# Attention and two MLPs on one core: values in two scaled fp16 parts, raw loads on POOL's queue, a lag of four

## The chip, the cores and the metric

The kernel runs on 1 core of a Trainium2 chip. The metric is the device time of one execution in microseconds (us), from the host's single launch; lower is better. The engines are named as the profile names them: PE (TensorE matmul), PEld (TensorE weight load), DVE (VectorE), ACT (ScalarE), POOL (GpSimd) and SP (SyncE, which here only issues transfers).

## The reference, cut to what matters

```python
# q, k, v: (4, 8, 576, 64) float32; s: (4, 8, 576)
scores = 1/sqrt(64) * q @ k.T                       # per batch and head
bias = minimum(-(cum[i] - cum[j]), 0)               # cum = cumsum(max(s, 0))
scores = where(j > i, -1e9, scores + bias)
attn = exp(scores - rowmax); attn /= sum(attn) + 1e-9
x = (attn @ v) -> (2304 tokens, 512)
h = x @ moe_w_in   (512 x 2048);  x = (h * tanh(softplus(h))) @ moe_w_out
h = x @ moe2_w_in  (512 x 2048);  out = (h * sigmoid(1.702 h)) @ moe2_w_out
```

The weights of both MLPs come as 8-byte numbers, which the kernel turns into float32 itself.

## The kernel before

Every product is made from parts of lower precision: a float32 operand is split into a high part and a remainder, and the partial products are added in PSUM.

**Attention.** There are 4 batches `b` of 8 heads, and 5 row tiles `i` per batch (four of 128 rows and one of 64, which takes two heads at a time). A *step* is a few heads of one row tile (`steps`, 104 of them, 26 a batch; 2, 4, 8, 8 and 4 steps for `i` = 0 to 4). A *group* is `(b, i, half of the heads)`, 40 of them; its raw keys, queries and values are loaded by `load_group` (three transfers, L133, on SP's queue) and prepared by `split_items`: PE transposes (L157), ACT and DVE split into parts.

`tick()` emits one step: scores (`do_qk`, L289 and L294 on PE), row minimum with the bias (`do_max`, L307 on DVE), `do_exp` (L111 on ACT), `do_hilo`, which splits the scaled probabilities into two fp16 parts (L333 ACT, L334 DVE) and transposes both by a DMA transpose on SP's queue (L338, tile `pt`). It also emits some items of the prepare queue `prep_q` for later groups, and then `do_av` of the step that lies `LAG` ticks back. The load of group `gi + 3` and the preparing of group `gi + 2` are emitted while group `gi` runs.

In `do_av` the values are there in three bf16 parts (L187 ACT, L189 DVE, L193 ACT, L194 POOL). For each 128 keys and head the high part of the probabilities is multiplied with all three parts (L357, 192 columns) and the low part with the first two (L361, 128 columns): 480 such pairs in all. The outputs of two heads share a PSUM bank, the only one of pool `ps_o`; L366 (DVE) adds the parts of each pair of heads. After the last step of a tile `norm_tile` divides by the sums (L379, L380 DVE, L381 POOL), and `emit_tile` transposes and splits the tile into the first MLP's input `xh`, `EDEL` ticks later.

**First MLP, first layer, among the ticks.** Unit `u` is 256 tokens. `first_layer` runs 16 blocks of weights on a unit (L530 to L532, three products a weight tile), and `slot_a` emits ticks between them, spread evenly. The first unit can start when its 256 tokens are done. A weight tile is loaded by `load_w` (L499 for the first layer, 512 KB, on SP's queue) and split by ACT, DVE and POOL (L514 to L526); loads begin after the fourth tick, one a tick. The last two units run after attention.

**The rest.** From about 443 us on come the second layer of the first MLP (L530 to L532 with `acc`) and the second MLP (L792). They are not touched by the change.

The framework puts each engine's instructions in an order of its own (by readiness in its own model, among those whose buffers are free) and inserts the waits; at run time each engine and each issuing queue works in that order.

Of the kernel before, what the change touches and what calls it, by code (L numbers as in the profile page):

```python
# [16 lines left out]
DRAM = bass.MemoryType.DRAM  # L17
BIG = 1.0e9
PSC = 32768.0
PH = 3  # L20
PS_ = 4
PO = 1
QW = 2
VB = 11
MA = 5
MBB = 4
NRAW = 2
LGC = 3
HLB = 3
PB = 2  # L30
RB = 1
XTB = 2
PTB = 4
WAH = 4
ES = 6
PG = 4
WT = 3
XH = 3
UE = 2
# [4 lines left out]
A0 = 4  # L44
A1 = 11
EDEL = 4
LAG = 3


@with_exitstack  # L50
def attention_moe_moe_kernel(
# [65 lines left out]
    def switch_set(name):  # L117
# [3 lines left out]
        del since[:]  # L121
        gate_ins[0] = p.ins


    raw = {}
# [23 lines left out]
    def split_items(b, i, g):  # L149
        n = min(128, S - 128 * i)  # L150
        hold = {}

        def flip(src, nm, off):
            ps = ps_s.tile([128, 512], F32, tag="s", name=nm)
            for hl in range(HG):
                o = hl * 128 + off(hl)
                nc.tensor.transpose(ps[:, o:o + n], src[:n, hl].rearrange("p w d -> p (w d)"), ident[:n, :n])  # L157
            return ps.rearrange("p (h t) -> p h t", h=HG)

        def kT():  # L160
# [23 lines left out]
        def v1():  # L184
            vr = raw[b, i, g][2]
            vt[b, i, g] = vv = v_p.tile([128, HG, 3, D], BF16, tag="v", name="v")
            nc.scalar.activation(out=vv[:n, :, 0, :], in_=vr[:n], func=AF.Copy)  # L187
            hold["vr"] = t = pp.tile([128, HG, D], F32, tag="res", name="res", bufs=RB)
            nc.vector.tensor_tensor(out=t[:n], in0=vr[:n], in1=vv[:n, :, 0, :], op=ALU.subtract)  # L189

        def v2():
            vv, t = vt[b, i, g], hold["vr"]
            nc.scalar.activation(out=vv[:n, :, 1, :], in_=t[:n], func=AF.Copy)  # L193
            nc.gpsimd.tensor_tensor(out=vv[:n, :, 2, :], in0=t[:n], in1=vv[:n, :, 1, :], op=ALU.subtract)  # L194
            raw.pop((b, i, g))

        return [qT, v1, v2], kT

    def cum_setup():
        NB = B * H  # L200
# [123 lines left out]
    def do_hilo(x):  # L324
        L, mu, nb = x["L"], x["mu"], x["nb"]
        Lp = nb * 128
        w = mu * Lp
        hl = pp.tile([128, 2 * NTIL * 128], F16, tag="hl", name="hl", bufs=HLB)
        hv = hl[:, 0:2 * w].rearrange("p (a w) -> p a w", a=2)
        if Lp != L:  # L330
            nc.gpsimd.memset(hv[:, :, L:Lp], 0.0)
        wl = mu * L
        nc.scalar.activation(out=hv[:, 0, 0:wl], in_=x["P"][:, 0:wl], func=AF.Copy, scale=PSC)  # L333
        nc.vector.scalar_tensor_tensor(  # L334
            out=hv[:, 1, 0:wl], in0=x["P"][:, 0:wl], scalar=PSC, in1=hv[:, 0, 0:wl], op0=ALU.mult, op1=ALU.subtract
        )
        x["T"] = d = pt_p.tile([128, 2 * NTIL, 128], F16, tag="pt", name="pt")
        nc.sync.dma_start_transpose(out=d[:, 0:2 * mu * nb, :], in_=hl[:, 0:2 * w])  # L338

    ohold = {}  # L340

    def do_av(x):
        b, i, g, n, mu, nb = x["b"], x["i"], x["g"], x["n"], x["mu"], x["nb"]
        t = x["T"]
        for e, hs in enumerate(x["hs"]):
            j = x["j"] + e
            if j % 2 == 0:
                ohold["o"] = ps_o.tile([128, 2, 256], F32, tag="o", name="o")
            o = ohold["o"]
            two = len(hs) == 2  # L350
            for kb in range(i + 1):
                kn = min(128, S - 128 * kb)
                for a, h in enumerate(hs):
                    hl = h - g * HG
                    rows = slice(64 * a, 64 * a + n) if two else slice(0, 128)
                    vv = vt[b, kb, g][:kn, hl, :, :].rearrange("p c d -> p (c d)")
                    nc.tensor.matmul(  # L357
                        out=o[rows, j % 2, 0:3 * D], lhsT=t[:kn, e * nb + kb, rows], rhs=vv,
                        start=(kb == 0 and j % 2 == 0), stop=False, skip_group_check=True,
                    )  # L360
                    nc.tensor.matmul(  # L361
                        out=o[rows, j % 2, 0:2 * D], lhsT=t[:kn, (mu + e) * nb + kb, rows], rhs=vv[:, 0:2 * D],
                        start=False, stop=(kb == i), skip_group_check=True,
                    )
            if j % 2 == 1:
                nc.vector.tensor_reduce(  # L366
                    out=tl[b, i]["x"][:, j - 1:j + 1, :],
                    in_=o[:, :, 0:3 * D].rearrange("p u (c d) -> p u d c", c=3), axis=mybir.AxisListType.X, op=ALU.add,
                )

    xunit = {}
# [2 lines left out]
    def norm_tile(x):  # L374
# [4 lines left out]
        nc.vector.tensor_scalar(out=rs, in0=su, scalar1=1e-9, scalar2=PSC, op0=ALU.add, op1=ALU.mult)  # L379
# [25 lines left out]
        tok_done[0] = t0 + n  # L405

    prep_q = []
    late_k = {}

    def queue_prep(gi):  # L410
        if gi >= len(groups):
            return
        b, i, g = groups[gi]
        items, kT = split_items(b, i, g)
        if 0 < gi < len(groups) - 1:
            prep_q.append(lambda: load_group(*groups[gi + 1]))
        prep_q.extend(items)
        if i == 0 and b > 0:
            late_k[groups.index((b - 1, NTIL - 1, g))] = kT
        else:  # L420
            prep_q.append(kT)

    def pop_prep(m):
        for _ in range(min(m, len(prep_q))):
            prep_q.pop(0)()
# [6 lines left out]
    def tick():  # L432
# [12 lines left out]
        if t < NS:  # L445
# [7 lines left out]
            if last_of[gi] == t and x["i"] == NTIL - 1 and x["b"] + 1 < B:  # L453
                load_ck(x["b"] + 1, x["g"])
            do_hilo(x)
        pop_prep(npop)
        while avn[0] < NS and t - avn[0] >= LAG:
            x = steps[avn[0]]
# [7 lines left out]

    def attn_left():
        return nxt[0] < NS + LAG + EDEL

    tmp_n = [0]  # L470
    mo_b = [None]

    def tmp_pair(dt, nm):
        tmp_n[0] += 1
        p = mo_a if mo_b[0] is None or tmp_n[0] % (MA + MBB) < MA else mo_b[0]
        return p.tile([128, 1024], dt, tag="hs", name=nm)


    win_t, wout_t = {}, {}
# [4 lines left out]
    def load_w(pool, stage, lay, m, kind):  # L484
# [11 lines left out]
            src = (w1_in, w2_in, w1_out, w2_out)[lay + 2 * (kind == "out")]  # L496
        if kind == "in":
            n = src.shape[1] // NF
            nc.sync.dma_start(  # L499
                out=rv.rearrange("p (c f) -> p c f", c=KC),  # L500
                in_=src[:, m * n:(m + 1) * n].rearrange("(c p) f -> p c f", p=128),
            )
            win_t[lay, m] = t
        else:
            nc.sync.dma_start(out=rv, in_=src[m * 128:(m + 1) * 128, :])
# [52 lines left out]
    for g in range(2):  # L558
        load_ck(0, g)

    queue_prep(0)
    pop_prep(len(prep_q))
    queue_prep(1)
# [288 lines left out]
```

## Time and profile before

| | |
|---|---|
| Median of 3 runs | 1086.47 us (1085.53 to 1091.34) |
| Profiled execution, its own time | 1086.05 us |
| Span of the profiled execution | 1084.3 us |
| PE busy over the span | 1009.3 us (93%) |
| DVE, ACT, POOL busy | 582.8, 495.0, 231.0 us |
| Mean granted PE clock | 0.974 |

The span runs from the first to the last recorded instruction; 1.75 us of the execution's own time lie outside it. A busy share says how long an engine had an instruction in it. Register, branch and transfer-issuing instructions are not counted as busy; a transfer's issue shows as SPq or POOLq.

### The profile page before, as it was taken

How to read it: one execution, taken by the hardware profiler on the slowest of the kernel's cores; microseconds unless marked ns; L12 is line 12 of the kernel's file. 1: busy time of each engine (PE TensorE's matmuls, PEld its weight loads, DVE VectorE, ACT ScalarE, POOL GpSimd, SP SyncE). 2: the span in 40 equal slices, each digit the busy share in tenths (PEclk: the TensorE clock that was granted, in tenths of full speed). 3: DMA queues.
4: the chain of work that ended last, by engine and by line, in shares of the span. 5: the costliest groups of instructions: out<-in, count | busy, mean ns of one | idle time of the engine just before them, and what ended most of it. 6: DMA issues, size and time to landing. Idle time of an engine off the chain costs nothing. (4 is left out here: it accounts for less than half of the span.)

```text
span 1084.3 us, 16945 instructions
## 1 busy us (share of the span) xinstructions
PE 1009.3 (93%) x6392; PEld 877.5 (81%) x6392; DVE 582.8 (54%) x1090; ACT 495.0 (46%) x1050; POOL 231.0 (21%) x239
## 2 busy tenths in 40 slices
PE   4488799989998999999999998799999999999998
PEld 4477689879987888998888878688888888888897
DVE  6979776665555974676644566773322232232231
ACT  6768676676656973455312343442222222222221
POOL 4414220112010211566423254230100100100000
PEclk9598999999999999999999998899999999999999
DMA  9669977996599778689534565530300210210010
GB/s 252 147 157 239 208 169 147 185 230 153 129 176 207 164 165 201 216 308 388 183 129 137 165 194 166 175 116 1 117 1 1 78 40 1 59 39 1 20 40 20
DMA packets 236913, 149.63 MB, mean 138 GB/s; under 512 B 166880, under 2 KB 210912, under 8 KB 236832
## 3 DMA queue, kind: packets, MB, share of 16 engines
q1 hardware_dynamic: 231392, 139.12, 48.7%
q0 software_dynamic: 5440, 9.44, 3.0%
q8 instruction: 50, 0.82, 0.3%
q14 instruction: 31, 0.25, 0.1%
HBM read 89.20 MB, written 33.10 MB: 113 GB/s over the span
## 5 line engine op out<-in xcount | busy, mean ns | idle before, releaser
L530 PE MATMUL h<-xh,w 128*128 128x256 f32 (+1 forms) x768 | 249.5, 328 | 6.7 <-DVE z L779 5.4
L531 PE MATMUL h<-xh,w 128*128 128x256 f32 (+1 forms) x768 | 247.4, 322 | 0.0
L532 PE MATMUL h<-xh,w 128*128 128x256 f32 (+1 forms) x768 | 246.4, 322 | 1.0 <-POOL w L526 1.0
L792 PE MATMUL acc<-w,gh 128*128 128x512 f32 x576 | 177.6, 389 | 0.0
L530 PEld LDWEIGHTS h<-xh,w 128*128 128x128 f32 x768 | 145.5, 191 | 19.2 <-DVE z L779 5.9
L532 PEld LDWEIGHTS h<-xh,w 128*128 128x128 f32 x768 | 146.7, 191 | 11.6 <-POOL w L526 1.4
L531 PEld LDWEIGHTS h<-xh,w 128*128 128x128 f32 x768 | 146.6, 191 | 10.5
L779 DVE TENSOR_TENSOR z<-h,sg 128x512 f32<-128x512 f32 x72 | 49.7, 691 | 190.6 <-ACT sg L111 190.2
L111 ACT ACTIVATE sg<-h 128x512 f32<-128x512 f32 x72 | 42.9, 596 | 202.8 <-PE h L532 202.8
L792 PEld LDWEIGHTS acc<-w,gh 128*128 128x128 f32 x576 | 107.6, 188 | 21.9
L531 PE MATMUL acc<-gl,w 128*128 128x512 f32 (+1 forms) x320 | 118.9, 372 | 6.1 <-DVE gl L665 6.0
L526 POOL TENSOR_TENSOR w<-wst,w 128x512 fp32r<-128x512 f32 x64 | 90.8, 1420 | 143.3 <-ACT w L525 137.6
L530 PE MATMUL acc<-gh,w 128*128 128x512 f32 (+1 forms) x320 | 118.5, 371 | 0.0
L532 PE MATMUL acc<-gh,w 128*128 128x512 f32 (+1 forms) x320 | 116.9, 371 | 0.1
L792 PE MATMUL acc<-w,gl 128*128 128x512 f32 x288 | 112.0, 389 | 0.0
L111 ACT ACTIVATE P<-P,mx 128x128 f32<-128x128 f32 (+4 forms) x144 | 83.5, 581 | 34.1 <-DVE mx L307 33.5
L334 DVE SCALAR_TENSOR_TENSOR hl<-P,hl 128x512 f16<-128x512 f32 (+2 forms) x104 | 74.8, 720 | 39.8 <-ACT hl L333 39.3
L357 PE MATMUL o<-v,pt 128*128 128x192 bf16 (+2 forms) x480 | 73.0, 257 | 23.5 <-DMA pt<-hl 13.4
L289 PE MATMUL s<-kw,qw 128*128 128x288 f32 (+4 forms) x384 | 90.3, 347 | 2.0 <-DVE qw L180 1.0
L514 ACT ACTIVATE wst<-wst 128x512 f32<-128x512 f32 x64 | 43.7, 683 | 77.2 <-DMA wst<-in_moe_w_out_dram 39.0
L781 DVE TENSOR_TENSOR gl<-z,gh 128x512 fp32r<-128x512 f32 x72 | 50.5, 701 | 47.8 <-ACT gh L780 35.7
L531 PEld LDWEIGHTS acc<-gl,w 128*128 128x128 f32 x320 | 61.4, 192 | 17.2 <-DVE gl L665 7.3
(79 smaller groups left out, 1713.0 us busy)
## 6 DMA issues: line engine op xcount, KB each, us to landing
h_d<-hs SPq DMA_DIRECT2D x36, 512.0 KB, 3.8
hg<-h_d SPq DMA_DIRECT2D x36, 512.0 KB, 6.3
wst<-in_moe_w_in_dram SPq DMA_DIRECT2D x32, 512.0 KB, 4.4
wst<-in_moe_w_out_dram SPq DMA_DIRECT2D x32, 512.0 KB, 3.7
x_d<-x SPq DMA_DIRECT2D x36, 256.0 KB, 2.8
xh<-x_d POOLq DMA_DIRECT2D x16, 512.0 KB, 5.2
cp<-cum_d SPq DMA_DIRECT2D x16, 288.0 KB, 5.1
ck<-cum_d SPq DMA_DIRECT2D x6, 768.0 KB, 6.9
```

The lines of the kernel that those rows point to most:

```text
L111: i = nc.scalar.activation(out=out, in_=in_, func=func, **kw)
L289: nc.tensor.matmul(out=o, lhsT=qw[b, i, g][:, hl, w, :], rhs=kw[b, g][:, hl, c0:c1], start=(e == a == w == 0), stop=False, skip_group_chec ...
L334: nc.vector.scalar_tensor_tensor(out=hv[:, 1, 0:wl], in0=x["P"][:, 0:wl], scalar=PSC, in1=hv[:, 0, 0:wl], op0=ALU.mult, op1=ALU.subtract)
L357: nc.tensor.matmul(out=o[rows, j % 2, 0:3 * D], lhsT=t[:kn, e * nb + kb, rows], rhs=vv, start=(kb == 0 and j % 2 == 0), stop=False, skip_g ...
L514: nc.scalar.activation(out=y, in_=y, func=AF.Copy, scale=2.0 ** -112)
L526: nc.gpsimd.tensor_tensor(out=tl_, in0=y, in1=th, op=ALU.subtract)
L530: nc.tensor.matmul(out=outp, lhsT=hi_w, rhs=hi_x, start=start, stop=False, skip_group_check=True)
L531: nc.tensor.matmul(out=outp, lhsT=hi_w, rhs=lo_x, start=False, stop=False, skip_group_check=True)
L532: nc.tensor.matmul(out=outp, lhsT=lo_w, rhs=hi_x, start=False, stop=stop, skip_group_check=True)
L779: nc.vector.tensor_tensor(out=z, in0=ps, in1=sg, op=ALU.mult)
L781: nc.vector.tensor_tensor(out=gl, in0=z, in1=gh, op=ALU.subtract)
L792: nc.tensor.matmul(out=acc[tb], lhsT=gx[:, ts], rhs=w[:, wx, :], start=m == 0 and a == 0, stop=m == NF - 1 and a == 2, skip_group_check=True,)
```

## The change

- The values are kept in two fp16 parts, after being scaled by a factor per batch that brings the batch's largest absolute value to 16384. `norm_tile` takes the factor out again. The factor needs the whole batch's values: `vscale_load(b)` loads them once more in three chunks of 128 x 768 floats into slots of the `hs` buffers and takes their largest (DVE), and `vscale_set(b)` makes the factor (a PE transpose and small DVE operations). For batch 0 they come at the start, for the others as items of the prepare queue with groups `(3, 0)` and `(4, 0)` of the batch before.
- `do_av` multiplies the high probabilities with both parts (128 columns) and the low ones with the first (64 columns). Four heads share the PSUM bank, and one reduction on DVE serves four heads.
- The remainder of the values is one DVE operation; one ACT, one DVE and one POOL operation per group fall away. Within a group keys are prepared ahead of values; the values of the first two groups are split after the first step.
- `load_group` issues its three transfers from POOL's queue instead of SP's from the fifth group on (`PG = 4`).
- `LAG` goes from 3 to 4, the `pt` buffers from 4 to 5, the value tiles from 11 to 12, the raw value buffers from 2 to 3; the buffer `res` goes.
- A weight load of the first layer is ordered on SP's queue behind the last transpose emitted before it.

```diff
-            t = pp.tile([128, HG, w, D], F32, tag=nm, name=nm, bufs=3 if nm == "kraw" else 2)
-            nc.sync.dma_start(
+            t = pp.tile([128, HG, w, D], F32, tag=nm, name=nm, bufs=2 if nm == "qraw" else 3)
+            (nc.sync if groups.index((b, i, g)) < PG else nc.gpsimd).dma_start(
...
-            vt[b, i, g] = vv = v_p.tile([128, HG, 3, D], BF16, tag="v", name="v")
-            nc.scalar.activation(out=vv[:n, :, 0, :], in_=vr[:n], func=AF.Copy)
-            hold["vr"] = t = pp.tile([128, HG, D], F32, tag="res", name="res", bufs=RB)
-            nc.vector.tensor_tensor(out=t[:n], in0=vr[:n], in1=vv[:n, :, 0, :], op=ALU.subtract)
+            vt[b, i, g] = vv = v_p.tile([128, HG, 2, D], F16, tag="v", name="v")
+            nc.scalar.activation(out=vv[:n, :, 0, :], in_=vr[:n], func=AF.Copy, scale=vsc[b][:n, 0:1])
...
-            nc.scalar.activation(out=vv[:n, :, 1, :], in_=t[:n], func=AF.Copy)
-            nc.gpsimd.tensor_tensor(out=vv[:n, :, 2, :], in0=t[:n], in1=vv[:n, :, 1, :], op=ALU.subtract)
+            nc.vector.scalar_tensor_tensor(
+                out=vv[:n, :, 1, :], in0=raw.pop((b, i, g))[2][:n], scalar=vsc[b][:n, 0:1], in1=vv[:n, :, 0, :],
+                op0=ALU.mult, op1=ALU.subtract,
+            )
...
+    def vscale_load(b):
+        flat = v[b].rearrange("h t d -> (h t d)").rearrange("(p n) -> p n", p=128)
+        vmx[b] = m = sm_p.tile([128, VC + 1], F32, tag="vm", name="vm")
+        for c in range(VC):
+            t = tmp_pair(F32, "vl")[:, 0:VW]
+            nc.sync.dma_start(out=t, in_=flat[:, c * VW:(c + 1) * VW])
+            nc.vector.tensor_reduce(
+                out=m[:, c:c + 1], in_=t, axis=mybir.AxisListType.X, op=ALU.max, apply_absolute_value=True
+            )
...
-            if j % 2 == 0:
-                ohold["o"] = ps_o.tile([128, 2, 256], F32, tag="o", name="o")
+            if j % 4 == 0:
+                ohold["o"] = ps_o.tile([128, 4, 2 * D], F32, tag="o", name="o")
...
+            if lay == 0 and last_pt[0] is not None:
+                tc.add_manual_dep(ld.ins, last_pt[0].ins.name, order, reason="weights behind transposes")
...
+    vscale_load(0)
     queue_prep(0)
```

## Rows read from the trace of the kernel before

**Rows 1.** Windows by stage: length, busy us and count per engine, clock, DMA share, GB/s.

```profile
0.00:122.00 122.00, 83.63 (x589) 72.70 (x590) 101.19 (x216) 85.44 (x204) 44.62 (x55) 0.86 0.83 200
122.00:140.00 18.00, 11.11 (x132) 9.34 (x129) 10.78 (x37) 11.03 (x34) 1.55 (x3) 0.91 1.03 203
140.00:443.00 303.00, 288.96 (x2640) 266.17 (x2641) 192.60 (x494) 200.18 (x515) 47.97 (x65) 0.99 0.78 172
443.00:600.00 157.00, 156.91 (x811) 134.76 (x810) 93.12 (x97) 59.19 (x77) 78.48 (x64) 1.00 0.67 232
```

**Rows 2.** Waits of PE, 0 to 445 us: total us, times, longest.

```profile
PE qt L157 <- ACT qraw L141: 18.2, 7, 6.7
PE o L357 <- DMA pt<-hl: 13.4, 9, 2.9
PE qt L157 <- POOL qraw L139: 11.9, 4, 5.2
PE o L357 <- DVE x L366: 10.1, 6, 2.9
```

**Rows 3.** Timeline of PE at 160 us: start, duration, instruction.

```profile
160.04 0.25 PE L357 MATMUL o<-v,pt 128*128 128x192 bf16 x1
160.12 0.22 PE L361 MATMUL o<-v,pt 128*128 128x128 bf16 x1
160.17 0.25 PE L357 MATMUL o<-v,pt 128*128 128x192 bf16 x1
```

**Rows 4.** Windows of L361 alone: PE and PEld busy us (count), clock, DMA share, GB/s.

```profile
140.00:443.00 303.00, 49.25 (x360) 30.66 (x360) 0.99 0.78 172
...
200.00:240.00 40.00, 7.55 (x64) 4.76 (x64) 1.00 0.98 210
...
320.00:360.00 40.00, 6.38 (x56) 3.97 (x56) 1.00 0.93 200
```

**Rows 5.** Windows of 40 us, columns as in Rows 1.

```profile
0.00:40.00 40.00, 17.63 (x90) 15.68 (x90) 30.31 (x65) 26.87 (x67) 16.44 (x29) 0.89 0.95 241
40.00:80.00 40.00, 29.95 (x221) 25.93 (x222) 30.78 (x70) 26.11 (x67) 9.99 (x10) 0.77 0.51 125
80.00:120.00 40.00, 34.05 (x262) 29.18 (x262) 38.24 (x80) 31.17 (x69) 16.76 (x15) 0.91 1.01 230
...
200.00:240.00 40.00, 35.45 (x355) 31.93 (x354) 24.41 (x76) 26.07 (x68) 4.24 (x8) 1.00 0.98 210
...
320.00:360.00 40.00, 36.04 (x359) 33.22 (x358) 24.32 (x71) 27.07 (x76) 5.21 (x9) 1.00 0.93 200
```

**Rows 6.** Groups by line, whole span: busy us, mean ns, idle before.

```profile
L366 DVE TENSOR_REDUCE x<-o 128x128 f32<-128x384 f32 x72 | 39.7, 552 | 27.4 <-PE o L361 27.0
...
L194 POOL TENSOR_TENSOR v<-res,v 128x256 bf16<-128x256 f32 (+1 forms) x40 | 28.1, 703 | 103.3 <-ACT v L193 94.4 <-DVE x L366 4.0 <-PE s L294 3.1
...
L189 DVE TENSOR_TENSOR res<-vraw,v 128x256 f32<-128x256 f32 (+1 forms) x40 | 20.5, 512 | 12.5 <-POOL v L194 7.6 <-ACT v L187 4.3 <-issue 0.3
L193 ACT ACTIVATE v<-res 128x256 bf16<-128x256 f32 (+1 forms) x40 | 16.5, 411 | 3.6 <-DVE res L189 3.5
```

**Rows 7.** Issue durations by tile or line, ns: minimum, median, maximum.

```profile
L133 SPq DMA_DIRECT2D qraw<-in_q_dram x40: 368/532/1507, 1.7 to 378.2; - x40
...
L338 SPq DMA_TRANSPOSE pt<-hl x104: 1210/1284/6617, 24.4 to 422.2; - x104
...
L757 POOL DMA_DIRECT2D xh<-x_d x20: 716/716/922, 637.4 to 1024.1; - x20
```

**Rows 8.** Waits of POOL, 0 to 445 us.

```profile
POOL x L381 <- DVE x L366: 96.6, 17, 24.4
```

**Rows 9.** Timeline of SP at the start; first unit's first product.

```profile
5.94 1.05 SPq L499 DMA_DIRECT2D wst<-in_moe_w_in_dram  x2
...
24.42 3.94 SPq L338 DMA_TRANSPOSE pt<-hl  x1
...
L530 PE MATMUL h<-xh,w x64: 278/283/562, 66.3 to 121.6; 128*128 128x256 f32 x64
```

More of the change, by code (lines that the diff above doesn't have):

```diff
@@ L19 @@
 PSC = 32768.0
+VTOP = 16384.0
 PH = 3
@@ L23 @@
 QW = 2
-VB = 11
+VB = 12
 MA = 5
@@ L30 @@
 PB = 2
-RB = 1
 XTB = 2
-PTB = 4
+PTB = 5
 WAH = 4
@@ L36 @@
 PG = 4
+VT = 0
 WT = 3
@@ L46 @@
 EDEL = 4
-LAG = 3
+LAG = 4
 @with_exitstack
@@ L122, in switch_set, with tmp_pair @@
         gate_ins[0] = p.ins
+    tmp_n = [0]
+    mo_b = [None]
+    def tmp_pair(dt, nm):
+        tmp_n[0] += 1
+        p = mo_a if mo_b[0] is None or tmp_n[0] % (MA + MBB) < MA else mo_b[0]
+        return p.tile([128, 1024], dt, tag="hs", name=nm)
     raw = {}
@@ L184, in v1 @@
         def v1():
+            if b not in vsc:
+                vscale_set(b)
             vr = raw[b, i, g][2]
-            vt[b, i, g] = vv = v_p.tile([128, HG, 3, D], BF16, tag="v", name="v")
-            nc.scalar.activation(out=vv[:n, :, 0, :], in_=vr[:n], func=AF.Copy)
-            hold["vr"] = t = pp.tile([128, HG, D], F32, tag="res", name="res", bufs=RB)
-            nc.vector.tensor_tensor(out=t[:n], in0=vr[:n], in1=vv[:n, :, 0, :], op=ALU.subtract)
+            vt[b, i, g] = vv = v_p.tile([128, HG, 2, D], F16, tag="v", name="v")
@@ L191, in v2 @@
+            nc.scalar.activation(out=vv[:n, :, 0, :], in_=vr[:n], func=AF.Copy, scale=vsc[b][:n, 0:1])
         def v2():
-            vv, t = vt[b, i, g], hold["vr"]
-            nc.scalar.activation(out=vv[:n, :, 1, :], in_=t[:n], func=AF.Copy)
-            nc.gpsimd.tensor_tensor(out=vv[:n, :, 2, :], in0=t[:n], in1=vv[:n, :, 1, :], op=ALU.subtract)
-            raw.pop((b, i, g))
-        return [qT, v1, v2], kT
+            vv = vt[b, i, g]
+            nc.vector.scalar_tensor_tensor(
+                out=vv[:n, :, 1, :], in0=raw.pop((b, i, g))[2][:n], scalar=vsc[b][:n, 0:1], in1=vv[:n, :, 0, :],
+                op0=ALU.mult, op1=ALU.subtract,
+            )
@@ new lines, in split_items @@
+        return [qT], [v1, v2], kT
+    vsc, vmx = {}, {}
+    VC = 3
+    VW = H * S * D // 128 // VC
+    def vscale_load(b):
[7 more added lines that the diff above has]
+            )
+        nc.vector.tensor_reduce(out=m[:, VC:VC + 1], in_=m[:, 0:VC], axis=mybir.AxisListType.X, op=ALU.max)
@@ new lines, in vscale_set @@
+    def vscale_set(b):
+        m = vmx.pop(b)
+        w = pp.tile([128, 128], F32, tag="vw", name="vw", bufs=1)
+        nc.vector.tensor_copy(w, m[:, VC:VC + 1].to_broadcast([128, 128]))
+        ps = ps_s.tile([128, 512], F32, tag="s", name="vx")
+        nc.tensor.transpose(ps[:, 0:128], w, ident)
+        vsc[b] = t = sm_p.tile([128, 2], F32, tag="vs", name="vs")
+        nc.vector.tensor_reduce(out=t[:, 0:1], in_=ps[:, 0:128], axis=mybir.AxisListType.X, op=ALU.max)
+        nc.vector.tensor_scalar(
+            out=t[:, 0:1], in0=t[:, 0:1], scalar1=1.0e-30, scalar2=1.0 / VTOP, op0=ALU.max, op1=ALU.mult
+        )
+        nc.vector.reciprocal(t[:, 0:1], t[:, 0:1])
+        nc.vector.tensor_scalar(out=t[:, 1:2], in0=t[:, 0:1], scalar1=PSC, scalar2=None, op0=ALU.mult)
@@ L337, in do_hilo @@
         x["T"] = d = pt_p.tile([128, 2 * NTIL, 128], F16, tag="pt", name="pt")
-        nc.sync.dma_start_transpose(out=d[:, 0:2 * mu * nb, :], in_=hl[:, 0:2 * w])
+        last_pt[0] = nc.sync.dma_start_transpose(out=d[:, 0:2 * mu * nb, :], in_=hl[:, 0:2 * w])
     ohold = {}
+    last_pt = [None]
     def do_av(x):
@@ L357, in do_av @@
                     nc.tensor.matmul(
-                        out=o[rows, j % 2, 0:3 * D], lhsT=t[:kn, e * nb + kb, rows], rhs=vv,
-                        start=(kb == 0 and j % 2 == 0), stop=False, skip_group_check=True,
+                        out=o[rows, j % 4, :], lhsT=t[:kn, e * nb + kb, rows], rhs=vv,
+                        start=(kb == 0 and j % 4 == 0), stop=False, skip_group_check=True,
                     )
                     nc.tensor.matmul(
-                        out=o[rows, j % 2, 0:2 * D], lhsT=t[:kn, (mu + e) * nb + kb, rows], rhs=vv[:, 0:2 * D],
+                        out=o[rows, j % 4, 0:D], lhsT=t[:kn, (mu + e) * nb + kb, rows], rhs=vv[:, 0:D],
                         start=False, stop=(kb == i), skip_group_check=True,
                     )
-            if j % 2 == 1:
+            if j % 4 == 3:
                 nc.vector.tensor_reduce(
-                    out=tl[b, i]["x"][:, j - 1:j + 1, :],
-                    in_=o[:, :, 0:3 * D].rearrange("p u (c d) -> p u d c", c=3), axis=mybir.AxisListType.X, op=ALU.add,
+                    out=tl[b, i]["x"][:, j - 3:j + 1, :],
+                    in_=o.rearrange("p u (c d) -> p u d c", c=2), axis=mybir.AxisListType.X, op=ALU.add,
                 )
@@ L378, in norm_tile @@
         su = ts["sums"]
-        nc.vector.tensor_scalar(out=rs, in0=su, scalar1=1e-9, scalar2=PSC, op0=ALU.add, op1=ALU.mult)
+        nc.vector.tensor_scalar(out=rs, in0=su, scalar1=1e-9, scalar2=vsc[x["b"]][:, 1:2], op0=ALU.add, op1=ALU.mult)
         nc.vector.reciprocal(rs, rs)
@@ L407, in attention_moe_moe_kernel @@
     prep_q = []
+    v_first = []
     late_k = {}
+    VSTEP = {(3, 0): vscale_load, (4, 0): vscale_set}
     def queue_prep(gi):
@@ L420, in queue_prep @@
         else:
-            prep_q.append(kT)
+            items = items + [kT]
+        if gi < 2:
+            v_first.extend(vs)
+        else:
+            items = items + vs
+        if b + 1 < B and (i, g) in VSTEP:
+            items = items + [lambda: VSTEP[i, g](b + 1)]
+        prep_q.extend(items)
     def pop_prep(m):
@@ L455, in tick @@
             do_hilo(x)
+        if t == VT:
+            for f in v_first:
+                f()
         pop_prep(npop)
```

11 lines of the change are left out of this document (2 added, 9 removed).

## The prediction, on record before the result

> **What bounds the kernel now.** I read first the windows by stage, to find where PE, which is busy for 93% of the span, has room, and where another resource is full; then PE's waits inside the attention stage, PE's timeline for the pace of the products that the change shortens, and SP's and POOL's queues, between which transfers move.
>
> The change touches the attention stage alone, 0 to 443 us. Behind it PE is busy for 156.91 of the next 157 us, and the stages after that have no code of the change; I take them as shifted whole. So the question is how much earlier 443 us comes.
>
> That stage has two regimes [rows 1]. From 140 to 443 us PE is busy for 289.0 of 303 us at a granted clock of 0.99, with DVE at 193, ACT at 200 and the transfer engines at 0.78: PE bounds it, and 14 us are idle. From 0 to 140 us PE is busy for only 94.7 of 140 us. There the transfers are nearly full: 0.83 x 122 + 1.03 x 18 = 120 us of 140; DVE has 112. In finer slices the transfers are at 0.95 in the first 40 us, 0.51 in the next, 1.01 in the third, while DVE reaches 38.2 of 40 in the third [rows 5]. The half-idle second slice says that order and latency, not volume alone, hold the start. Two more slices, around the batch ends, look like the start: 200 to 240 (transfers 0.98, PE 35.45) and 320 to 360 (0.93, 36.04) [rows 5].
>
> PE's waits in the stage are few and named: for raw queries by way of the copies on ACT (18.2 us) and POOL (11.9), for `pt` from the DMA transpose (13.4), for the one `o` bank (10.1) [rows 2]. All four lie on things that the change moves.
>
> **The products, term one.** In the timeline a pair starts at 160.04, its second half at 160.12, the next pair at 160.17 [rows 3]: 0.13 us for 192 + 128 columns, which is one column a cycle at the 2.4 GHz level (133 ns: 80 and 53). After the change a pair is 128 + 64 columns. The 128-column half takes 53 ns instead of 80, a sure 27 ns. The 64-column half would be 27 ns by columns, but no row shows a 64-column product before another of this kind; if the weight load in front of each product sets a floor, that floor is at most the 53 ns that a 128-column one takes. So a pair saves 27 to 53 ns. I take 45: PEld is busy for 30.7 us over these 360 L361 loads [rows 4], 85 ns each, and two of them fit in the 133 ns of a pair only overlapped, so they have not been the limit, but how far below they go isn't seen.
>
> The Trainium skill ("TensorE: Matmul & The Clock Gate", Back-to-back issue gap) says that in a stream of weight load and product pairs a 128-column product takes about 81 ns. By it the new pair could hardly be under the old 133 ns, and this term would be nothing. The row shows 53 ns at 128 columns, so I go by the row.
>
> 360 of the 480 pairs lie behind 140 us, 64 and 56 of them in the two full slices at the batch ends [rows 4]. There, and for the 120 pairs of the first 140 us, PE isn't the bound and shorter products give no time. That leaves 240 x 45 ns = 11 us; if the batch ends gain too, 360 x 53 ns = 19 us; at the least, 240 x 27 ns = 6 us.
>
> **SP's queue and the waits, term two.** 36 groups x 3 = 108 issues leave SP. One takes 532 ns [rows 7], 57 us in all, and they stand in order with 104 transposes of 1.28 us (133 us). Each raw load ahead of a transpose holds it by its own issue and by whatever the load waits for. With a lag of four a transpose may also land one tick later. Of the 14 us that PE idles behind 140 us I give back 3; none to 8 bound it. The `o` bank now changes hands once for four heads.
>
> **The start, term three.** Today two weight tiles are issued at 5.94 us, ahead of most raw loads, and the first transpose's issue takes 3.94 us instead of the usual 1.28 because the transfers are full [rows 7, 9]. The new order puts all weight loads of the first layer behind transposes, and raw loads from the fifth group on leave SP. Against it: batch 0's values are read twice at the start. A batch is 8 x 576 x 64 x 4 B = 1.18 MB, 4.9 us at the 241 GB/s of the first slice [rows 5]; batch 1's second reading (b = 0, group (3, 0)) also falls before 140 us, so transfers rise from 120 to about 130 us. And the first unit starts one tick later: today's first product of it is at 66.3 us [rows 9], ten ticks in, so a tick is at most some 6 us, whose work isn't lost, since later ticks then have less. Best case: the stretch shrinks from 140 to the 130 us that its transfers need, 10 us. Worst: the two readings and a tick in full, 16 us lost. I take 6 us gained: the raw-query waits, 30 us in all [rows 2], of which at least 16 lie here since PE idles only 14 us later, come from the loads and copies that queue behind weights, and the 0.51 slice has room for the weights moved there.
>
> **The other engines, nothing.** ACT loses L193, 16.5 us; POOL loses L194, 28.1 us [rows 6]; none of it is on PE's path behind 140 us. DVE: 72 reductions of 552 ns over 384 elements become 36 over 512; by elements 736 ns, so 26.5 instead of 39.7 us. L189 is replaced by one operation on as many elements, 0.5 us as before. Twelve reductions over 768 elements cost 0.55 to 1.1 us each, 7 to 13 us, and the small operations for four factors perhaps 4 us, an estimate from five of about 0.2 us each. Together between -2 and +4 us on an engine that is 64% busy behind 140 us [rows 1]. PE gets four more transposes. If the cover of DVE's room were gone, as between 80 and 120 us, 4 us is what it costs.
>
> POOL takes 108 issues. The only ones in the trace take 716 ns [rows 7], 77 us; a raw load has shorter runs, so up to twice that, 155 us. POOL has 94 us of work in 443 today [rows 1], less 28, so 143 to 221 us afterwards: it fits, but in order. Behind each issue that waits for a raw buffer stand L526 (weights), L381 (normalising) and the memsets; and the loads stand behind these.
>
> The remaining readings of the values (b = 2, 3) are 2 x 4.9 us of transfers in the stretch whose mean share is 0.78 [rows 1], issued ahead of the full slices at the batch ends; I cost them at nothing as long as they land there, and at 10 us if they don't.
>
> **Sum.** Against the profiled execution's own 1086.05 us: 11 + 3 + 6 = 20 us less, 1066 us. The median shown is 1086.47, 0.4 above; the difference is inside rounding. A measurement of this kernel can tell about 0.5%, 5.4 us, from no change.
>
> **Rivals.**
> - *Raw loads come late from POOL (slower).* POOL stands at L381 for DVE's reduction 17 times, 96.6 us in all, up to 24.4 us in one [rows 8]. A raw load behind such a wait comes late, and PE then waits at the transposes (L157) as it does today at the start. It decides from 20/36 = 0.56 us of lateness per group on; at 0.8 us per group, 29 us, the time is 1066 + 29 = 1095. Against it: loads are emitted some three groups ahead, and a group is about 11 us (443/40), so a wait must be far longer than the usual 5.7 us (96.6/17) to matter. The Trainium skill ("DMA: Bandwidth & Descriptors", SWDGE vs HWDGE vs iDMA) adds that POOL writes its descriptors into SBUF, where DVE can lock it out; no row here prices that. 10%.
> - *Transfers are the bound after all.* Four readings, 4.7 MB, at 241 GB/s are 19.6 us; if they all fall into full stretches, they eat the gain: 1066 + 19.6 = about 1086. For it: four slices at 0.93 or more [rows 5]. Against: two of the four readings lie between the full stretches. 12%.
> - *The pair does not get shorter*, the floor being the weight load's: term one is nothing, and 1086 - 9 = 1077. Against: the 53 ns pace. 9%.
> - *More than forecast*: 19 us from the products, 8 from waits, 10 from the start: 1049. 9%.
> - *As forecast*, 1052 to 1078: 60%.
>
> The forecast and the two faster rivals lie below 1081, the transfers' case about the same as now, POOL's case above 1092: faster 0.78, same 0.12, slower 0.10. Leaving out the slower case and the outer half of the best one, and keeping the transfers' case, the range is 1049 to 1088.
>
> **What would show it.** Right: L357 and L361 pairs spaced at 80 to 110 ns; PE still above 95% behind the start; the first product of unit 0 no later than 66 us; the attention stage ending near 423 us. Wrong: PE idle in front of L157 for many groups with POOL's issue as what came last (the slower rival); transfers above 0.9 through the whole stage with waits for `pt` (the second); pairs at 130 ns (the third). A long wait for the scale factor of batch 0 before the first products with values would also undo the start's term.

## The result and the profile after

The changed kernel takes 1075.67 us (median of 7 runs, 1072.73 to 1080.59) against 1085.94 (7 runs) for the kernel before on the same chip: a ratio of 0.9896, 95% interval 0.9876 to 0.9916, so 1.04% or 11.3 us faster. Forecast was 1066, 20 us faster. The profiled execution took 1073.94 us.

Windows of the changed kernel by stage, columns as in [rows 1] (length, busy us and count of PE, PEld, DVE, ACT, POOL, clock, DMA share, GB/s), the last boundaries 10 us earlier than there:

```profile
0.00:122.00 122.00, 84.04 (x586) 71.82 (x587) 98.56 (x224) 78.77 (x189) 54.69 (x74) 0.78 0.95 219
122.00:140.00 18.00, 13.80 (x130) 11.61 (x128) 14.75 (x43) 16.29 (x47) 10.65 (x12) 0.91 1.09 252
140.00:433.00 293.00, 282.36 (x2703) 259.26 (x2703) 187.94 (x485) 194.47 (x483) 79.16 (x107) 0.99 0.85 189
433.00:590.00 157.00, 155.03 (x776) 131.76 (x775) 89.17 (x97) 58.72 (x75) 72.08 (x63) 1.00 0.64 225
```

POOL's busy time in these rows includes its issues of raw loads; on this engine, unlike on SP, an issue is counted as busy. PE is still the bound behind 140 us (282.4 of 293), but the transfers went from 0.83 to 0.95 in the first 122 us and from 0.78 to 0.85 behind them. The slices of 40 us, which answer to [rows 5], show where:

```profile
0.00:40.00 40.00, 20.91 (x120) 18.73 (x120) 26.82 (x72) 22.81 (x63) 18.48 (x36) 0.76 0.77 192
40.00:80.00 40.00, 29.05 (x205) 23.95 (x206) 36.33 (x74) 27.91 (x65) 14.94 (x16) 0.73 1.00 230
80.00:120.00 40.00, 32.08 (x245) 27.58 (x245) 35.08 (x80) 27.72 (x62) 20.62 (x23) 0.83 1.03 233
120.00:160.00 40.00, 35.80 (x346) 32.31 (x346) 31.55 (x82) 32.28 (x90) 19.37 (x24) 0.96 1.04 232
200.00:240.00 40.00, 36.24 (x365) 32.66 (x365) 27.32 (x83) 29.87 (x81) 14.16 (x22) 0.96 1.02 220
```

The half-empty slice of before (0.51 from 40 to 80 us) is gone: from 40 to 160 us the transfers are full without a gap. The fullness that stood in single slices has become one block, while the first slice fell from 0.95 to 0.77. PE is granted 0.78 of its clock over the first 122 us instead of 0.86 (both are means of the two levels), though it is as busy there as before, 84.0 us against 83.6; no run tells why.

PE's timeline of the changed kernel, to be held against [rows 3]:

```profile
170.16 0.22 PE L397 MATMUL o<-v,pt 128*128 128x128 f16 x1
170.22 0.19 PE L401 MATMUL o<-v,pt 128*128 128x64 f16 x1
170.25 0.22 PE L397 MATMUL o<-v,pt 128*128 128x128 f16 x1
170.30 0.19 PE L401 MATMUL o<-v,pt 128*128 128x64 f16 x1
```

The starts are 60, 30 and 50 ns apart. Over the pairs from 150 to 405 us that are followed at once by another one, the median spacing is 85 ns (164 pairs, halves of 57 and 28 ns; mean 89), where the kernel before has 138 ns (159 pairs, 83 and 56; mean 141): 53 ns less a pair.

PE's waits from 0 to 445 us in the changed kernel, columns as in [rows 2]:

```profile
PE o L397 <- DMA pt<-hl: 15.7, 11, 6.5
PE qt L166 <- POOL qraw L148: 5.2, 1, 5.2
...
PE o L397 <- DVE x L406: 3.3, 3, 2.9
PE qt L166 <- ACT qraw L150: 1.6, 2, 0.9
```

The waits for raw queries fell from 30.1 to 6.8 us and the one for the `o` bank from 10.1 to 3.3; the one for `pt` stayed (13.4 to 15.7). What the attention stage gave the later ones is seen in the line of the last two units' first layer, which run behind attention, before and after:

```profile
L530 PE MATMUL acc<-xh,w x128: 278/283/386, 424.8 to 472.7; 128*128 128x256 f32 x128
L576 PE MATMUL acc<-xh,w x128: 277/283/386, 408.7 to 456.2; 128*128 128x256 f32 x128
```

It begins at 408.7 us; in the kernel before at 424.8. The first product of the second MLP comes at 685.3 instead of 697.9, and the span ends at 1072.2 instead of 1084.3. So attention is 16.1 us shorter in the two profiles, and 3.6 us of them are lost again between the last two units and the second MLP, where no code changed.

### The profile page after: what moved, and what is told of

Its sections match the earlier page's. It is cut to its first block, busy times and chain, and to the rows that moved or that the text cites. A ratio compares the mean times of both kernels' runs of the same rounds, so it can differ in the third digit from the quotient of the medians.

```text
span 1072.2 us, 16959 instructions
## 1 busy us (share of the span) xinstructions
PE 1001.4 (93%) x6396; PEld 866.1 (81%) x6396; DVE 568.2 (53%) x1090; ACT 485.6 (45%) x1010; POOL 275.7 (26%) x307
## 4 chain that ended last, share of the span: by engine, by line
PE 49%; DMA 7%; DVE 4%; POOL 3%; issue 3%; ACT 2%; SPq 0%; ACTq 0%; POOLq 0%; DVEq 0%
PE acc L839 18%; PE h L576 7%; PE h L577 7%; PE h L578 7%; PE acc L578 3%; PE acc L577 3%; PE acc L576 3%; DMA wst<-in_moe_w_out_dram 2%; DMA wst<-in_moe_w_in_dram 2%; POOL w L572 2%; DMA x_d<-x 1%; DVE wst L565 1%; DVE gl L712 1%; DVE wst L562 1%; DMA kraw<-in_k_dram 1%
## 5 line engine op out<-in xcount | busy, mean ns | idle before, releaser
L576 PEld LDWEIGHTS h<-xh,w 128*128 128x128 f32 x768 | 147.7, 194 | 22.6 <-DVE z L826 6.1
L578 PEld LDWEIGHTS h<-xh,w 128*128 128x128 f32 x768 | 148.5, 193 | 11.5 <-POOL w L572 1.1
L577 PEld LDWEIGHTS h<-xh,w 128*128 128x128 f32 x768 | 148.5, 193 | 11.0 <-DVE xh L443 0.2
L112 ACT ACTIVATE P<-P,mx 128x128 f32<-128x128 f32 (+4 forms) x144 | 83.6, 582 | 32.4 <-DVE mx L346 31.9
L804 POOL DMA_DIRECT2D xh<-x_d x20 | 14.5, 729 | 285.3 <-PE h L578 197.4
L373 DVE SCALAR_TENSOR_TENSOR hl<-P,hl 128x512 f16<-128x512 f32 (+2 forms) x104 | 71.5, 688 | 30.5 <-ACT hl L372 30.2
L346 DVE CUSTOM_DVE_ANT_0 P<-s,ck 128x128 f32<-128x128 f32 (+3 forms) x128 | 59.2, 486 | 30.5 <-PE s L333 29.4
```

Source lines behind the costliest of these rows:

```text
L112: i = nc.scalar.activation(out=out, in_=in_, func=func, **kw)
L346: nc.vector.tensor_tensor_reduce(out=p[:, e * L + c0:e * L + c1], in0=x["S"][f][:, e * L:e * L + c1 - c0], in1=c[:, c0:c1], scale=1.0, sca ...
L373: nc.vector.scalar_tensor_tensor(out=hv[:, 1, 0:wl], in0=x["P"][:, 0:wl], scalar=PSC, in1=hv[:, 0, 0:wl], op0=ALU.mult, op1=ALU.subtract)
L576: nc.tensor.matmul(out=outp, lhsT=hi_w, rhs=hi_x, start=start, stop=False, skip_group_check=True)
L577: nc.tensor.matmul(out=outp, lhsT=hi_w, rhs=lo_x, start=False, stop=False, skip_group_check=True)
L578: nc.tensor.matmul(out=outp, lhsT=lo_w, rhs=hi_x, start=False, stop=stop, skip_group_check=True)
```

## The experiments

The theory after the result: the products and the queue gave what they could, and the second reading of the values, costed inside the start and at nothing for batches 2 and 3, ate the difference. The rivals: the products gave less than 11 us; the raw loads came late from POOL; the lag of four or the weight order cost something. Ratios are to the kernel before on the same chip (medians of 1089.16, 1086.97 and 1087.85 us in the three groups); differences of ratios are turned into us with 1087. The change itself was run only beside its own kernel before, so every comparison with it goes by way of that kernel. An interval reaches 0.002 to 0.004 to either side, so a difference is good to some 3 to 5 us.

| kernel | median, us | ratio, 95% |
|---|---|---|
| the change | 1075.67 | 0.9896 [0.9876, 0.9916] |
| e1_raw_on_sp | 1086.18 | 0.9977 [0.9957, 0.9996] |
| e2_low_part_128 | 1084.26 | 0.9968 [0.9950, 0.9986] |
| e3_no_second_reading | 1060.94 | 0.9746 [0.9713, 0.9779] |
| e4_lag3 | 1085.32 | 0.9952 [0.9926, 0.9978] |
| e5_no_weight_order | 1075.93 | 0.9903 [0.9877, 0.9930] |
| e6_before_raw_on_pool | 1083.47 | 0.9960 [0.9945, 0.9974] |
| e8_products_alone | 1089.78 | 1.0025 [1.0009, 1.0040] |
| e9_four_chunks | 1074.24 | 0.9873 [0.9837, 0.9909] |
| e12_transfers_only | 1072.20 | 0.9841 [0.9815, 0.9866] |
| e13_reduces_only | 1066.97 | 0.9796 [0.9766, 0.9827] |
| e14_products_no_reading | 1066.66 | 0.9808 [0.9788, 0.9828] |
| e10_constant_lag5 | 1059.26 | 0.9749 [0.9722, 0.9777] |

**Raw loads back on SP's queue.** The changed kernel, the lag and the rest kept.

```diff
-            (nc.sync if groups.index((b, i, g)) < PG else nc.gpsimd).dma_start(
+            nc.sync.dma_start(
```

> All raw loads go back to SP's queue; the rest of the change stays. Theory (transfers bound the start, PE the rest, and taking 108 issues from SP's queue is worth a few us of waits): the final units start 2 to 6 us later than in the changed kernel (408.7 us there), mostly lost behind 140 us, and the time is 1077 to 1082 us. Rival (raw loads come late from POOL and that is where the missing gain went): the final units start 4 us or more earlier and the time is below 1072 us.

It is 0.81% or 8.8 us slower than the change (0.9977 against 0.9896), more than the theory expected. The raw loads didn't come late from POOL; there they save time. What they cost is seen in the landings of the transposes, 0 to 440 us, by tile: issuing queue, form, count, median us from issue to landing. This kernel first, then the changed one:

```profile
pt<-hl SPq DMA_TRANSPOSE x104, 3.5
```

```profile
kraw<-in_k_dram POOLq DMA_DIRECT2D x28, 128.0 KB, 5.8
...
pt<-hl SPq DMA_TRANSPOSE x104, 4.2
```

With two queues at work a transpose lands 0.7 us later, and a raw load in 4.5 to 5.8 us (values to keys) instead of 3.0 to 3.4 in the kernel before. In exchange SP more often stands ready at a transpose and waits only for its data. The waits for that, in the kernel before, in this one and in the changed one:

```profile
SPq L338 <- DVE hl L334: 43.8, 35, 4.1
...
SPq L377 <- DVE hl L373: 34.4, 28, 3.2
...
SPq L377 <- DVE hl L373: 101.7, 60, 6.3
```

**The low part's product with 128 columns again.** It multiplies the low probabilities with both value parts.

```diff
-                        out=o[rows, j % 4, 0:D], lhsT=t[:kn, (mu + e) * nb + kb, rows], rhs=vv[:, 0:D],
+                        out=o[rows, j % 4, :], lhsT=t[:kn, (mu + e) * nb + kb, rows], rhs=vv,
```

> The low probabilities are again multiplied with both parts of the values, 128 columns instead of 64, on PE alone. Theory (PE bounds the stage from 140 us on, one column a cycle): the pair goes from about 95 to about 120 ns, the start of unit 1 stays at 142 +- 2 us, and 240 to 360 pairs x 27 ns make the final units start 6 to 10 us later. Rival (the gain came from the lag, the queue and the waits, not from the products): the final units move by less than 2 us.

0.72% or 7.8 us slower than the change, within the theory's 6 to 10 us (in its profile the last two units start 14.0 us later). The pair takes 112 ns (median) instead of 85. If every one of the 360 pairs behind 140 us were on the path, 27 ns each would make 9.6 us, and 240 of them 6.4; good to some 3 us, the run can't tell the two apart.

**No second reading.** The factor is a constant; the three loads and their reductions are left out. This holds for values below about 3 in magnitude only.

```diff
         vmx[b] = m = sm_p.tile([128, VC + 1], F32, tag="vm", name="vm")
-        for c in range(VC):
...
-        nc.vector.tensor_reduce(out=m[:, VC:VC + 1], in_=m[:, 0:VC], axis=mybir.AxisListType.X, op=ALU.max)
+        nc.vector.memset(m, 0.75)
```

> The values are scaled by a constant, and the second reading of them with its reductions is left out: 4.7 MB of transfers and 12 DVE operations less. Theory (transfers at a share of 1.0 from 40 to 160 us bound the start, and the two readings that fall there cost about 4.9 us each): unit 1 starts 5 to 10 us earlier than 142.4 us, the final units 5 to 12 us earlier, the time is 1064 to 1071 us. Rival (the readings are hidden, the start is held by the attention chain itself): unit 1 starts within 2 us of 142.4.

1060.94 us, 1.5% or 16.3 us faster than the change, more than the theory expected. The second reading is the largest cost of the change. In the profiles this kernel leads by 2.8 us at the start of unit 1, by 6.1 at the last two units and by 10.8 at the end of the span; 4.0 us of it come between the last two units and the second MLP, where nothing is read.

Where the third and the fourth reading land, the transfers become full and, in the second of these windows, PE is busy for 7.79 of 10 us instead of all of it (single profiles both). The windows from 152 to 163 and from 263 to 273 us, columns as in [rows 1], in the changed kernel and then in this one:

```profile
152.00:163.00 11.00, 11.00 (x108) 10.43 (x108) 8.77 (x19) 6.61 (x19) 2.99 (x4) 1.00 1.08 269
263.00:273.00 10.00, 7.79 (x85) 7.12 (x84) 5.25 (x10) 4.75 (x10) 1.05 (x2) 1.00 0.97 239
...
152.00:163.00 11.00, 11.00 (x108) 10.47 (x107) 7.17 (x17) 8.30 (x21) 1.97 (x3) 1.00 0.67 158
263.00:273.00 10.00, 10.00 (x100) 9.51 (x99) 5.60 (x13) 6.79 (x16) 2.40 (x3) 1.00 0.60 151
```

**A lag of three**, with four `pt` buffers.

```diff
-PTB = 5
+PTB = 4
...
-LAG = 4
+LAG = 3
```

> Lag of three and four transposed buffers as before the change; the rest of the change stays. Theory (the lag is worth little): unit 0 starts up to 4 us earlier, since it needs one tick less, unit 1 within 3 us, the final units within 3 us of 408.7. Rival (the longer lag is what made the waits for transposes shorter and so brought much of the gain): the final units start 5 us or more later and PE waits for transposes 10 us more than the 15.7 us of the changed kernel.

0.56% or 6.1 us slower than the change, as the rival said. PE's waits of this kernel, 0 to 445 us, go with it: the wait for transposes is 33.2 us, where the changed kernel has 15.7.

```profile
PE o L397 <- DMA pt<-hl: 33.2, 23, 5.8
```

That later landings make a lag of three too short is not shown by that: the kernel before with its raw loads on POOL's queue (below) also has a lag of three and transposes that land in 3.9 us, as they do here, and waits 16.6 us for them.

**No weight order.** Weight loads of the first layer aren't ordered behind transposes.

```diff
-            if lay == 0 and last_pt[0] is not None:
+            if False:
```

> The order of weight loads behind transposes is taken out; the rest of the change stays. Theory (the order only moves transfers from the first 40 us to the next, both full now): unit 0 starts 2 to 6 us later than at 61.4 us, unit 1 within 3 us of 142.4, the final units within 4 us of 408.7. Rival (the parts only work together, as taking out the lag or the queue alone cost 10 to 11 us at the final units): the final units start 8 us or more later.

0.9903 against 0.9896: nothing. The first layer's first product comes at 74.4 us here and at 61.4 in the change, but unit 1 starts at 142.5 and 142.4. Thirteen us gained at 60 us are worth nothing at 142. In this run unit 0's products are done at 125.3 us and unit 1 begins 17 us later, so the start of unit 0 is not on the path; what holds unit 1 no run tells.

**The queue alone, on the kernel before.** Raw loads from POOL's queue from the fifth group on, nothing else.

```diff
-            nc.sync.dma_start(
+            (nc.sync if groups.index((b, i, g)) < PG else nc.gpsimd).dma_start(
```

> The kernel before with one part of the change alone: raw loads from POOL's queue from the fifth group on. If each part has a price of its own, this one is worth the 10 us that its removal cost (final units at 414 to 417 us instead of 424.8). If the parts only work together (products on PE and the transposes in front of them bind in turn), it alone brings under 4 us, because PE is still busy for 95% of the stretch behind 140 us. If raw loads come late from POOL, it is slower.

0.4% or 4.3 us faster than before, half of the 8.8 us that the queue is worth in the change. It falls between the cases expected. The lag of three isn't the reason for the half, as the next run shows, and the difference is at the edge of what the runs can tell.

**The products with the reading, nothing else.** The change with a lag of three, raw loads on SP, no weight order. It also keeps what comes with the products: keys prepared before values, the bank of four heads.

```diff
-PTB = 5
+PTB = 4
...
-LAG = 4
+LAG = 3
...
-            (nc.sync if groups.index((b, i, g)) < PG else nc.gpsimd).dma_start(
+            nc.sync.dma_start(
...
-            if lay == 0 and last_pt[0] is not None:
+            if False:
```

> The changed kernel with lag three, raw loads on SP's queue and no order of the weight loads: what stays is the values in two fp16 parts with their second reading, the shorter products and the key preparing ahead of values. If each part has a price of its own: 14 us of products less 6 us of second reading, final units at about 417 us. If the parts only work together: under 4 us gained or a loss, final units at 421 us or later.

1.0025 [1.0009, 1.0040]: no gain at all. The arithmetic of the change, with the reading that it needs, pays nothing by itself; lag, queue and order make the 1.3% (14 us) between this kernel and the change.

With the order worth nothing, four kernels now show lag and queue singly and together. The queue is worth 8.8 us at a lag of four and 7.9 at a lag of three (0.9952 against 1.0025); the lag is worth 6.1 us with the raw loads on POOL's queue and 5.2 with them on SP's (0.9977 against 1.0025). As far as these runs can tell, each is worth the same without the other.

**Four chunks instead of three.** The same bytes and elements in 16 transfers and reductions instead of 12.

```diff
-    VC = 3
+    VC = 4
```

> The second reading of the values in four chunks of 576 floats instead of three of 768: the same bytes, nearly the same work. It is there to see how far a change of almost nothing moves the order in which the framework puts the later instructions, and with it the times: final units within 2 us of 408.7 if the scatter is small. The stretch from the final units to the second MLP's first products (276.6 us in the changed kernel, 273.0 before) has no part of the change in it: theory (its order is drawn anew by any change): it lies between 272 and 280 us. If it stays within 1 us of 276.6, something of the change itself lengthens it.

0.9873 [0.9837, 0.9909], not to be told from the change: the number of pieces costs nothing that can be seen. Yet in its profile unit 1 starts 5.4 us later and the last two units 7.4 us later than in the changed kernel's (147.8 and 416.1 us). Single profiles of nearly the same kernel differ by that much at such a mark, so marks less than some 7 us apart, those above included, prove nothing here; what is said of times goes by ratios.

**The transfers without the reductions.** The three loads stay, DVE copies one column of each, the factor is a constant.

```diff
-            nc.vector.tensor_reduce(
-                out=m[:, c:c + 1], in_=t, axis=mybir.AxisListType.X, op=ALU.max, apply_absolute_value=True
-            )
-        nc.vector.tensor_reduce(out=m[:, VC:VC + 1], in_=m[:, 0:VC], axis=mybir.AxisListType.X, op=ALU.max)
+            e = sm_p.tile([128, 1], F32, tag="ve", name="ve")
+            nc.vector.tensor_copy(e, t[:, 0:1])
+        nc.vector.memset(m, 0.75)
```

> The scale is a constant as in the run without the second reading, but the transfers of the second reading are kept (12 of 384 KB into the same slots, one DVE copy of a single column each); the reductions are left out and no value waits for a transfer. If the 15 us that the second reading costs are the transfers' (4.9 us of full transfer time for each batch): 1073 to 1077 us, as the changed kernel. If they are DVE's or the wait for the factor: 1060 to 1064 us.

**The reductions without the transfers.** They read a constant tile, and the factor comes out constant.

```diff
-            t = tmp_pair(F32, "vl")[:, 0:VW]
-            nc.sync.dma_start(out=t, in_=flat[:, c * VW:(c + 1) * VW])
+            t = ident[:, 0:1].to_broadcast([128, VW])
```

> The reductions, the small operations and the wait for the factor are kept, but the twelve reductions read 768 times a column of a constant tile, and the second reading's transfers are left out, so the factor is a constant. If the transfers are what costs: 1060 to 1064 us, as without the second reading. If DVE's 11.3 us of reductions or the chain to the factor cost: 1073 to 1077 us.

Against the kernel without any reading (0.9746) the transfers cost 0.95%, 10.3 us, good to some 5 us. In this kernel the loads also still take their 12 `hs` slots, which the 10.3 us include, and in its profile, a single one, 3.4 us of the 8.3 that it ends later come between the last two units and the second MLP, where no reading lies. The change is another 0.55%, 6.0 us, slower: that is what the reductions in their places and the wait for the factor cost, good to some 4 us.

The kernel with the reductions alone does not price them. With no load to wait for they all run in the first 12 us; in the change they are spread. By line: instruction, count, ns (minimum, median, maximum), first and last start, in the change and in this kernel:

```profile
L219 DVE TENSOR_REDUCE vm<-vl x12: 939/950/954, 9.2 to 272.3; 128x1 f32<-128x768 f32 x12
...
L218 DVE TENSOR_REDUCE vm<-ident x12: 930/935/940, 1.8 to 11.6; 128x1 f32<-128x768 f32 x12
```

Its 0.50%, 5.4 us, is the price of twelve reductions in one go at the start, and that it and the 10.3 come near the whole 16.3 shows nothing.

**The products alone, without the reading.** The kernel of the products with the reading, and this on top; the factor is a constant, the reading and its reductions are left out.

```diff
-        for c in range(VC):
...
-        nc.vector.tensor_reduce(out=m[:, VC:VC + 1], in_=m[:, 0:VC], axis=mybir.AxisListType.X, op=ALU.max)
+        nc.vector.memset(m, 0.75)
```

> The products alone (lag three, raw loads on SP's queue, no order of weight loads), with a constant scale and without the second reading. With the second reading this was 2.7 us slower than before. If the reading costs its 15 us here too: 1072 to 1076 us, a gain of 11 to 15 us over before, which is then what shorter products bring by themselves (11 forecast). If the shorter products bring nothing without the lag and the queue: 1082 us or more.

0.9808: 1.92% or 20.9 us faster than before, more than the 11 to 15 expected. The rival that the products gave less than forecast has fallen; with what comes with them (operations that fall away on ACT, DVE and POOL, the bank of four heads, keys ahead of values) they give nearly twice as much. Against the products with the reading (1.0025) it also prices the reading a second time: 2.2%, 23.6 us, with raw loads on SP and a lag of three. So lag, queue and order together take 7 us off the price of the reading.

**A lag of five**, on the kernel without the second reading, with six `pt` buffers and eleven value tiles.

```diff
-VB = 12
+VB = 11
...
-PTB = 5
+PTB = 6
...
-LAG = 4
+LAG = 5
```

> Constant scale, no second reading, and a lag of five with six transposed buffers (11 value tiles instead of 12, to make room). If waits for transposes still cost PE time (24.5 us of them in the run without the second reading), 3 to 6 us less than that run's 1061: 1055 to 1058 us. If the lag is long enough at four, 1060 to 1064 us.

0.9749 against 0.9746 with four: nothing more. Without the reading a lag of four is long enough. Both kernels with the constant beat the change and the kernel before, for values of bounded size.

## Why the prediction was right in its sign and 10 us too far

The time lies in the range and in the forecast case's own 1052 to 1078 us, but two of the terms were badly sized, in opposite directions, so that it lies there is partly luck. Of the signs named for a right forecast three came: pairs within 80 to 110 ns (85), PE above 95% behind the start (96), the first product of unit 0 before 66 us (61.4). The fourth, the end of attention 20 us earlier, came to 16.

**Term one, the products: 11 us forecast, about 21 measured together with what came with them.** The pair saves 53 ns, the upper bound (138 to 85; the forecast took 133 for the old pair from three starts); the 64-column half isn't held at 53 ns by its weight load, the next product starts 28 ns after it. So the third rival is refuted, and with it what the back-to-back issue gap of the Trainium skill ("TensorE: Matmul & The Clock Gate") would have made of this term: products of 128 columns follow at 57 ns here, not 81. What failed in the step is probably the count: I left out the 120 pairs of the two full slices. 360 x 53 ns = 19.1 us lies within the 18.7 to 23.0 of the products alone, 240 x 53 ns = 12.7 us does not. This is argued, not shown: the operations that fell away on the other engines and the pairs of the first 140 us are in the 20.9 too, the run with 128 columns fits either count, and no run parts them.

**The second reading: the step that failed.** It stood inside term three for batches 0 and 1, and for batches 2 and 3 it read "I cost them at nothing as long as they land there, and at 10 us if they don't". All four cost 16.3 us by removal. The transfers with their slots make 10.3 us of it, half of the 19.6 that four readings last at 241 GB/s. The third and the fourth reading did land ahead of the full slices, and yet they were not free: they fell into windows whose share without them is 0.67 and 0.60, and filled them to 1.08 and 0.97. How the cost divides over the four batches no run tells. The other 6.0 us had been put under "the other engines, nothing": twelve reductions and what waits for them. This line of the changed kernel's groups, 0 to 440 us (busy us, mean ns, idle before), shows that the size of the reductions was right, 11.3 us within 7 to 13, and only their being covered was wrong:

```profile
L219 DVE TENSOR_REDUCE vm<-vl 128x1 f32<-128x768 f32 x12 | 11.3, 948 | 3.9 <-DMA vl<-in_v_dram 3.8
```

A fuller DVE doesn't explain it by itself: over the first 122 us it is busy for 98.6 us, before the change for 101.2. Which wait carries the 6.0 us stays open.

The transfers' rival, given 12%, named the right resource but not the price: the whole reading came to 16.3 us against its 19.6, the transfers with their slots to 10.3. Its sign, transfers above 0.9 through the whole stage with waits for `pt`, didn't come: behind 140 us they are at 0.85, and the waits are 15.7 us against 13.4. What kept the reading from deciding is that the products with what came with them gave more.

**Terms two and three, waits and start: 9 us forecast, 7 to 14 measured**, and not where I put them. The start term, 6 us: the first product of unit 0 came 4.9 us earlier as forecast (61.4 against 66.3), but unit 1 only 2.1 us earlier (142.4 against 144.5), which single profiles can't tell from nothing; the weight order, which I counted on, is worth nothing. The lag and POOL's queue, which I gave 3 us, are worth 6.1 and 8.8 us when undone singly, and 14 with the order when undone together. Without the reading all three together make 6.7 us (0.9808 to 0.9746): half of what they give goes into covering the reading.

**POOL.** The slower rival is refuted by e1 and e6. An issue of a raw load takes hardly longer than the only ones that the kernel before had (716 ns, [rows 7]); the groups of the changed kernel, 0 to 440 us, have

```profile
L142 POOL DMA_DIRECT2D qraw<-in_q_dram x36 | 26.5, 735 | 74.2 <-PE qt L166 34.6 <-issue 14.0 <-ACT P L112 9.1
...
L406 DVE TENSOR_REDUCE x<-o 128x256 f32<-128x512 f32 x36 | 24.7, 685 | 12.0 <-PE o L401 11.5 <-PE xt L430 0.5
```

735 ns, near the lower of the two bounds. DVE's reductions of four heads take 24.7 us, where 26.5 were forecast. The wait behind which the loads were to come late shrank: POOL's wait at its normalising line is 31.7 us instead of 96.6 [rows 8]. The larger reductions aren't the reason. These are the same waits in the changed kernel with the raw loads back on SP's queue, which has the reductions of four heads too, in the kernel before with its raw loads on POOL's queue, and in the changed kernel:

```profile
POOL x L421 <- DVE x L406: 148.1, 17, 29.9
...
POOL x L381 <- DVE x L366: 38.0, 11, 11.0
...
POOL x L421 <- DVE x L406: 31.7, 12, 12.3
```

Moving the loads alone brings 96.6 us to 38.0, so most of the wait was time in which POOL had nothing else to do, and their issues now fill it.

**"The stages after that shifted whole."** Not quite: from the last two units to the second MLP the profiles have 273.0 us before and 276.6 after. All seven kernels that keep three loads a batch have 274.9 to 279.7, all six others with the old number of `hs` tiles (the kernel before, e3, e6, e10, e13, e14) 272.6 to 274.5, and e9 with four loads 271.0. The loads advance the counter by which the later splits choose their rotating buffers, and each engine's order there is redrawn. That is a correlation in single profiles; no run changed the counter alone, and it stays open.

From the kernel before by way of the products alone and the kernel without the reading to the change: 20.9 of the products with what came with them + 6.7 of lag, queue and order - 16.3 of the reading = 11.3 us. These are the steps of one chain from the kernel before to the change, so the sum comes out by construction and confirms nothing; in another order the steps have other sizes (-2.7 and 14.0 by way of the products with the reading).

Not tried: a lag of four alone on the kernel before, the weight order alone on it, the high part's product with 192 columns alone, and the other start of the buffer counter alone.

## What to carry to other kernels

Don't cost an added transfer at nothing because the mean share of its stretch has room: at a mean share of 0.78, 4.7 MB cost about 10 us (their buffer slots included) of the 19.6 that they last at the full rate, and the operations and waits that came with them another 6; two of the four readings landed in windows that they themselves filled. Don't write off PE work in a stretch that looks bound by something else; the products with what came with them gave 20.9 us where the count without such stretches gave 11. What a second queue and more lag are worth depends on what else the transfers carry: with the order of weights 6.7 us without the reading and 14 with it.

## What was unexpected of the hardware

- A 64-column fp16 product with a weight load of its own, between 128-column ones, is followed by the next after 28 ns (median), and a 128-column one after 57; the weight load sets no floor at 53.
- POOL's queue issues a load of 512 runs of 256 B in 735 ns (mean; median 749), hardly more than it takes for longer runs (716 ns), and moves them in far fewer packets: 4800 for 12.59 MB from 0 to 420 us, about 2.6 KB each. A transpose on SP's queue lands 0.4 to 0.7 us later beside it (3.5 to 3.9 at a lag of three, 3.5 to 4.2 at four).
- A gain of 13 us at the first layer's first product left nothing 80 us later.
